# Query tiles 2 to 4 in float16 parts, late products ordered behind the feed-forward part's, and two unread products more

## The chip, the core and the metric

The kernel runs on one core of a Trainium2 chip. The core's engines have instruction queues of their own, each worked off in order: TensorE (PE in the profile; its weight loads are PEld), VectorE (DVE), ScalarE (ACT), GpSimd (POOL), and SyncE (SP), which issues the DMAs. They wait for one another by semaphores. The metric is the device time of one execution in microseconds; lower is better.

## The reference

Linear attention with softmax-like features, then a feed-forward layer over the attention's output.

```python
q, k, v: (8, 8, 576, 64)   omega: (128, 64)   w_in: (512, 2048)   w_out: (2048, 512)
def phi(x):                      # x scaled by 64 ** -0.25
    h = einsum('bhsd,md->bhsm', x, omega) - sum(x * x) / 2
    return exp(h - max(h, axis=-1)) / sqrt(128)
q_p, k_p = phi(q_s), phi(k_s)
kv  = einsum('bhsm,bhsd->bhmd', k_p, v);  z = sum(k_p, axis=2)
att = einsum('bhsm,bhmd->bhsd', q_p, kv) / (einsum('bhsm,bhm->bhs', q_p, z) + 1e-6)
x   = att as (4608, 512)
h   = x @ w_in
out = (h * tanh(softplus(h))) @ w_out
```

## The kernel before

The 4608 rows are 36 query tiles of 128 rows (`q_task`, tile t) and 18 feed-forward chunks of 256 rows (two tiles each). Per batch element b there are four tasks `k_task` (two heads each), whose result `kv` a query tile needs, and one `v_task` that finds the scale of v. Every tile or chunk goes through a list of steps, and a slot counter with numbers written by hand (`FIRST`, `GAP`, `pace`, the `yield` values) sets in which order the steps are written out. A scheduler then sets each engine's final order from that; a waiting instruction holds all behind it on its engine.

**Two kinds of product.** A product is done either in float32 or in float16 parts: the operand is rounded to float16, the rest is kept as a second float16 array, and three products (or two, for the features) add up. In parts, TensorE has more instructions, each much shorter; the splitting costs work on the other engines.

**A query tile** t below `QF` (5) runs in float32: the features `pq` (L333), a maximum `mxq` on VectorE, eight exponentials on ScalarE with the maximum as bias (L347), eight transposes `pt` on TensorE (L528), copies `qp` on ScalarE, the products `pn` with the float32 `kvf` (L539). From `QF` on it runs in parts: `sq` = the rounded q (ScalarE, L68) and its rest (GpSimd, L77), `pq` from these, `mxq` and the subtraction `eq` (L351) on VectorE, one exponential (L357), its two parts `qn` (ScalarE, VectorE), a transpose by DMA `qp<-qn` (L471), the products `pn` (L485) with `kv`. Either way follow the division into `x` on VectorE, its parts `xs`, and a transpose by DMA into `xT` of its chunk; for tiles 0 and 1 instead transposes `px` on TensorE (L563) into a float32 `xT`.

**A key task** gives `pk` (L333), `ek`, and then `pkv`: for b = 0 and 1 (`KF` = 2) in float32 (L403), later in parts with `vb` (L435), whose rest part is GpSimd's. `kv_parts` splits the `kvf` of b = 0 or 1 into `kv` for tiles in parts; with `QF` = 5 only b = 1 needs it.

**The scales.** `pow2` takes a maximum over all partitions with GpSimd's `partition_all_reduce` (L110): `allm_v` once for each b, `allm_w` once for each of the two weights. Between that operation and an ordinary one on GpSimd the program has an `ISA` instruction that changes GpSimd's library.

**The feed-forward part.** `ff_in` gives the products `ph` (L626) into two PSUM buffers, emptied by ScalarE; `ff_out` the products `po` (L669, L686). Chunk 0 is float32 (`wi0`, `wo0`); meanwhile ScalarE and VectorE unpack the weights (`w_task`: the Prelu of L178, the maxima `wmax`, the Abs of L192) and split them (`w_split`), which chunk 1 and later need. `mish` needs another function table on ScalarE than the exponentials and the rest; `mish0` does chunk 0's in one piece.

**Unread products.** `spin(n, left, right)` issues n products that nobody reads. `ps_a`, four PSUM buffers, holds `pq`, `pk`, `pt`, `pn`, `pkv` and `px` in turn.

Of the kernel before, what the change touches and what calls it, by code (L numbers as in the profile page):

```python
# [2 lines left out]

# [7 lines left out]
F32 = mybir.dt.float32  # L11
# [18 lines left out]
def tile_kernel(  # L30
# [129 lines left out]
    @contextmanager  # L160
    def behind(nth):
        with ExitStack() as st:
            for ins in anchors.get(nth, ()):
                st.enter_context(tc.issue_after(ins))
            yield

    def w_task(i, name):

        n = 0 if name == "wi" else 1
        raw = loaded.pop(f"w{n}_{i}", None) or fetch_w(n, i, w_dma)  # L170
        yield W_LOAD
        word = raw.bitcast(I32).rearrange("p (n two) -> p n two", two=2)
        low, high = word[:, :, 0], word[:, :, 1]
        dst = flat32(slots[w_at(n, i)])
        di = dst.bitcast(I32)
        with behind((AN, AO)[n][i]):
            m = high.bitcast(F32)
            act.activation(m, m, AF.Prelu, scale=2.0 ** -112, alpha=-(2.0 ** 32))  # L178
            dve.tensor_single_scalar(out=di, in_=low, scalar=29, op=ALU.logical_shift_right)
        yield W_GAP  # L180
        did("w", n, i)
        with behind((AN, AO)[n][i]):
            dve.scalar_tensor_tensor(
                out=di, in0=high, scalar=3, in1=di, op0=ALU.logical_shift_left, op1=ALU.bitwise_or
            )
            if n == 0:
                dve.tensor_reduce(
                    out=wmax[n][:, i:i + 1], in_=dst, axis=AX.X, op=ALU.max, apply_absolute_value=True
                )
            else:  # L190

                act.activation(m, dst, AF.Abs, accum_out=wmax[n][:, i:i + 1])  # L192
# [100 lines left out]
    unit = [0]  # L293

    loaded = {}
    anchors = {}
# [15 lines left out]
    def features(load, tiles, name, nth, whole):  # L312

        f = loaded.pop(name, None) or fetch(load, name)
        yield gap("load", name)
        if whole:

            terms = ((f, om_f[0:D]),)  # L320
        else:
            terms = yield from in_parts(f, name, nth)
        n = sum(len(g) for g in tiles)
        by_act = whole
        e = sb.tile([P, n, M], F32, tag="ae", name=f"e{name}", bufs=2)
        mx = sb.tile([P, n], F32, tag="mx", name=f"mx{name}")
        pps, lo = [], 0
        for g in tiles:
            pp = ps_a.tile([P, 4, M], F32, tag="a", name=f"p{name}_{lo}")
            for i, parts in enumerate(g):  # L330
                for rows, o in parts:
                    for j, (left, right) in enumerate(terms):
                        nc.tensor.matmul(  # L333
                            out=pp[rows, i, :], lhsT=left[:, o:o + rows.stop - rows.start],
                            rhs=right, start=j == 0, stop=j == len(terms) - 1,
                        )
# [25 lines left out]

    kvf = {}
# [18 lines left out]
    def k_task(nth, b, hp):  # L382
# [46 lines left out]
        rest(by("vlo", nth), v_lo, va, v_hi, s_v)  # L429
        yield gap("kv", f"k{b}_{hp}")  # L430
        pkv = ps_a.tile([P, 2, D1], F32, tag="a", name=f"pkv{b}_{hp}", padded_shape=[P, 2, 256])
        for j in range(2):
            mm = [(t, u, x, y) for x, y in ((1, 0), (0, 1), (0, 0)) for t, u in steps[j]]
            for i, (t, u, x, y) in enumerate(mm):
                nc.tensor.matmul(  # L435
                    out=pkv[:, j, :], lhsT=kp[:, x, t, :], rhs=vv[:, y, u, :],
                    start=i == 0, stop=i == len(mm) - 1,
                )
# [16 lines left out]
    def q_task(nth, t):  # L455
# [15 lines left out]
        nc.sync.dma_start_transpose(  # L471
            out=qp.rearrange("p a h s -> p (a h) s"), in_=qn.rearrange("p a h m -> p (a h m)")
        )
        yield 2
        x = sb.tile([P, H, D], F32, tag="x", name=f"x{t}", bufs=2)
        rd = sb.tile([P, H, 1], F32, tag="rd", name=f"rd{t}")
        pns = []
        for g in range(2):
            pn = ps_a.tile([P, 4, D1], F32, tag="a", name=f"pn{t}_{g}", padded_shape=[P, 4, P])
            for i in range(4):  # L480
                h = 4 * g + i
                for b, lo, hi in spans(t * P, P):
                    must(HP, "kv", b)
                    for n, (a, y) in enumerate(((1, 0), (0, 1), (0, 0))):
                        nc.tensor.matmul(  # L485
                            out=pn[lo:hi, i, :], lhsT=qp[:, a, h, lo:hi], rhs=kv[b][:, h, y, :],
                            start=n == 0, stop=n == 2,
                        )
            pns.append(pn)
# [31 lines left out]
    def q_first(nth, t, e, off):  # L521
# [11 lines left out]
        for g in range(2):  # L533
# [9 lines left out]
            dve.tensor_single_scalar(out=rd[:, hs], in_=pn[:, :, D:D1], scalar=EPS, op=ALU.add)  # L543
            dve.reciprocal(out=rd[:, hs], in_=rd[:, hs])
            if t * P < CH:
                xt = dve.tensor_tensor(
                    out=x[:, hs, :], in0=pn[:, :, 0:D], in1=rd[:, hs].broadcast_to([P, 4, D]),
                    op=ALU.mult,
                )
# [12 lines left out]
        for i in range(KT):  # L562
            nc.tensor.transpose(out=px[:, i, :], in_=x[:, 2 * i:2 * i + 2, :], identity=ident)  # L563
# [43 lines left out]
    def ff_in(c):  # L607
# [3 lines left out]
        for gr in range(FT // FG):  # L611
            gT[c, gr] = sb.tile([P, 2, FG, CH], F16, tag="g", name=f"g{c}_{gr}", bufs=GB)
            for q in range(FG // FQ):
# [4 lines left out]
                for j in range(0, FQ, 2):  # L618
                    ph = ps_h.tile([P, 2, CH], F32, tag="h", name=f"ph{c}_{gr}_{q}_{j}")
                    for i in range(2):  # L620
# [2 lines left out]
                        if c == 0:  # L623
                            mm = [(None, None, k) for k in range(KT)]
                        for n, (a, y, k) in enumerate(mm):
                            nc.tensor.matmul(  # L626
                                out=ph[:, i, :], lhsT=wi(a, k, f) if c else wi0(k, f),
                                rhs=xT[c][:, y, k, :] if c else xT0()[:, k, :],
                                start=n == 0, stop=n == len(mm) - 1,
                            )  # L630
# [48 lines left out]
    def ff_out0():  # L679

        po = [ps_o.tile([P, DM], F32, tag="o", name=f"po0_{i}") for i in range(CH // P)]
        for blk in reversed(range(NB)):
            for i in range(CH // P):
                for f in (2 * blk, 2 * blk + 1):
                    must(f // FG + 1, "g", 0, f % FG // FQ)
                    nc.tensor.matmul(  # L686
                        out=po[i], lhsT=g0(f // FG)[:, f % FG, i * P:(i + 1) * P], rhs=wo0(f),
                        start=blk == NB - 1 and f % 2 == 0, stop=blk == 0 and f % 2 == 1,
                    )
# [218 lines left out]
```

## Time and profile before

| | |
|---|---|
| three runs | 990.11, 991.0 and 972.43 us; median 990.11 us |
| profiled execution | 972.64 us, span 970.9 us, mean granted TensorE clock 0.987 |
| TensorE busy | 953.8 us, 98% of the span |
| ScalarE, VectorE, GpSimd busy | 642.4, 529.6, 218.0 us |
| the costliest groups on TensorE | `ph` in parts 379.9 us (3264 products), `po` in parts 373.1 us (1632) |

A row of a timeline has the start in us, the duration, the engine, the line, the operation, what it writes and reads, the shape, and the number of instructions merged; in square brackets the engine's idle time before it and what ended that. A row of a table by stretches has the stretch, its length, then the busy time of PE, PEld, DVE, ACT and POOL with the number of instructions in brackets, the granted TensorE clock (1.00 is full speed), the DMA share and GB/s. A row of waits has who waited, for whom, the sum in us, how often, and the longest. A float32 product counts twice on TensorE in the trace and once in the program's order.

### The profile page before, as it was taken

To read this page: it belongs to the slowest core of one execution; us is meant where nothing else is said; L and a number is where in the kernel's file an instruction comes from. 1 tells how busy PE (TensorE), PEld (TensorE's weight loads), DVE (VectorE), ACT (ScalarE), POOL (GpSimd) and SP (SyncE) were. 2 spreads that over 40 slices of the span, in tenths; PEclk is the share of its full clock that TensorE was granted. 3 is DMA by queue.
4 is the path that set the end of the run, shared out by engine and by line. 5 is a ranking of instruction groups with operands and counts; after the bars stand their busy time and mean duration, and the time that the engine had idled before them with its cause. 6 is when DMAs were issued, how large, how long until landed. Compare 5 with 4: busy or idle time off the path is not lost.

```text
span 970.9 us, 19229 instructions
## 1 busy us (share of the span) xinstructions
PE 953.8 (98%) x8184; PEld 684.0 (70%) x8184; DVE 529.6 (55%) x945; ACT 642.4 (66%) x838; POOL 218.0 (22%) x135
## 2 busy tenths in 40 slices
PE   8999998998999999999999999999999999999998
PEld 6788874775777777777777777777777777766663
DVE  5868676585656655655465665565546555211110
ACT  4659995797676867777667775877667766232230
POOL 0000051243222422322132323332223130000000
PEclk9979998999999999999999999999999999999999
DMA  9756323432441245322422253312530124200000
GB/s 289 263 204 209 108 73 67 101 80 63 98 107 37 83 93 111 63 67 73 112 57 59 63 119 73 89 37 68 90 89 24 45 55 88 44 23 11 12 12 32
DMA packets 122245, 82.21 MB, mean 85 GB/s; under 512 B 102832, under 2 KB 102960, under 8 KB 122160
## 3 DMA queue, kind: packets, MB, share of 16 engines
q1 hardware_dynamic: 122160, 80.99, 33.3%
q8 instruction: 64, 1.05, 0.4%
q14 instruction: 21, 0.17, 0.1%
HBM read 46.37 MB, written 9.44 MB: 57 GB/s over the span
## 4 chain that ended last, share of the span: by engine, by line
PE 75%; DVE 1%; issue 0%; POOL 0%; ACT 0%; ACTq 0%
PE po L669 34%; PE ph L626 32%; PE pk L333 3%; PE pq L333 2%; PE pn L485 2%; PE pkv L435 2%; POOL vb L77 0%; DVE g L79 0%; DVE eq L351 0%; DVE mxq L342 0%; ACT o L68 0%; DVE vb L70 0%; DVE kv L79 0%; DVE p_v L117 0%; DVE s_v L119 0%
## 5 line engine op out<-in xcount | busy, mean ns | idle before, releaser
L626 PE MATMUL ph<-xT,w 128*128 128x256 f16 (+1 forms) x3392 | 413.3, 278 | 0.7 <-ACT xT L68 0.7
L669 PE MATMUL po<-wo,g 128*128 128x512 f16 x1632 | 373.1, 379 | 0.0
L626 PEld LDWEIGHTS <-w 128*128 128x128 f16 x3264 | 318.4, 98 | 59.7 <-issue 0.8
L669 PEld LDWEIGHTS <-g 128*128 128x128 f16 x1632 | 155.7, 98 | 163.6
L645 ACT ACTIVATE h<-ph,us 128x512 f32<-128x512 f32 (+3 forms) x184 | 101.1, 574 | 199.3 <-PE ph L626 198.5
L79 DVE SCALAR_TENSOR_TENSOR g<-h,us,g 128x1024 f16<-128x1024 f32 (+3 forms) x92 | 112.5, 1238 | 118.1 <-ACT g L68 117.7
L77 POOL TENSOR_TENSOR sq<-fq,sq 64x1024 f16<-64x1024 f32 x31 | 71.6, 2309 | 178.6 <-issue 100.4
L77 POOL TENSOR_TENSOR sk<-fk,sk 64x1152 f16<-64x1152 f32 x24 | 59.2, 2468 | 116.2 <-DVE mxq L342 27.6
L68 ACT ACTIVATE g<-h,us 128x1024 f16<-128x1024 f32 (+3 forms) x92 | 82.4, 923 | 1.2
L77 POOL TENSOR_TENSOR xs<-x,xs 128x512 f16<-128x512 f32 x32 | 42.5, 1328 | 141.9 <-ACT h L645 47.1
L342 DVE TENSOR_REDUCE mxq<-pq 128x4 f32<-128x512 f32 x72 | 46.9, 684 | 49.4 <-PE pq L333 49.3
L645 ACT ACT_TABLE_LOAD x55 | 70.6, 1283 | 1.0
L357 ACT ACT_TABLE_LOAD x53 | 68.0, 1283 | 0.9
L342 DVE TENSOR_REDUCE mxk<-pk 128x4 f32<-128x512 f32 (+1 forms) x96 | 50.3, 550 | 33.4 <-PE pk L333 33.4
L77 DVE TENSOR_TENSOR qn<-eq,qn 128x1024 f16<-128x1024 f32 x31 | 39.9, 1286 | 50.4 <-ACT qn L68 50.4
L77 DVE TENSOR_TENSOR kp<-ek,kp 128x1152 f16<-128x1152 f32 x24 | 37.7, 1570 | 21.0 <-ACT kp L68 21.0
L77 POOL TENSOR_TENSOR vb<-vf,vb 128x640 f16<-128x640 f32 x24 | 39.8, 1661 | 30.5 <-DVE vb L70 18.4
L68 ACT ACTIVATE o<-po,us 128x512 f32<-128x512 f32 (+1 forms) x38 | 25.9, 682 | 30.9 <-PE po L669 30.8
L281 DVE TENSOR_REDUCE vmx<-vf 128x1 f32<-128x640 f32 x32 | 25.9, 816 | 35.5 <-DMA vf<-in_vL_dram 35.4
L351 DVE TENSOR_TENSOR eq<-pq,mxq 128x512 f32<-128x512 f32 x62 | 39.9, 681 | 0.0
L357 ACT ACTIVATE eq<-eq,lnt 128x1024 f32<-128x1024 f32 x31 | 35.6, 1149 | 6.2 <-DVE eq L351 5.9
L357 ACT ACTIVATE ek<-ek,lnt 128x1152 f32<-128x1152 f32 x24 | 30.1, 1256 | 12.3 <-DVE ek L351 12.1
(124 smaller groups left out, 920.5 us busy)
## 6 DMA issues: line engine op xcount, KB each, us to landing
vf<-in_vL_dram SPq DMA_DIRECT2D x32, 325.0 KB, 3.3
fk<-in_kT_dram SPq DMA_DIRECT2D x32, 288.0 KB, 3.6
fq<-in_qT_dram SPq DMA_DIRECT2D x36, 256.0 KB, 3.5
out_dram<-o SPq DMA_DIRECT2D x36, 256.0 KB, 2.3
raw<-in_w_out_dram SPq DMA_DIRECT2D x5, 1024.0 KB, 9.2
wo<-in_w_in_dram SPq DMA_DIRECT2D x4, 1024.0 KB, 13.2
raw<-in_w_in_dram SPq DMA_DIRECT2D x4, 1024.0 KB, 15.3
wo<-in_w_out_dram SPq DMA_DIRECT2D x3, 1024.0 KB, 7.0
```

The lines of the kernel that those rows point to most:

```text
L68: act.activation(out, in_, AF.Copy, scale=scale)
L77: eng.tensor_tensor(out=out, in0=in_, in1=hi, op=ALU.subtract)
L79: eng.scalar_tensor_tensor(out=out, in0=in_, scalar=scale, in1=hi, op0=ALU.mult, op1=ALU.subtract)
L281: dve.tensor_reduce(out=mx[:, hp:hp + 1], in_=vt[hp][:, :, 0:D], axis=AX.XY, op=ALU.max, apply_absolute_value=True,)
L333: nc.tensor.matmul(out=pp[rows, i, :], lhsT=left[:, o:o + rows.stop - rows.start], rhs=right, start=j == 0, stop=j == len(terms) - 1,)
L342: sub = dve.tensor_reduce(out=mx[:, lo:hi], in_=pp[:, :m, :], axis=AX.X, op=ALU.max, negate=by_act)
L351: sub = dve.tensor_tensor(out=e[:, lo:hi, :], in0=pp[:, :m, :], in1=mx[:, lo:hi].unsqueeze(2).broadcast_to([P, m, M]), op=ALU.subtract,)
L357: last = act.activation(e, e, AF.Exp, bias=lnt)
L435: nc.tensor.matmul(out=pkv[:, j, :], lhsT=kp[:, x, t, :], rhs=vv[:, y, u, :], start=i == 0, stop=i == len(mm) - 1,)
L626: nc.tensor.matmul(out=ph[:, i, :], lhsT=wi(a, k, f) if c else wi0(k, f), rhs=xT[c][:, y, k, :] if c else xT0()[:, k, :], start=n == 0, st ...
L645: act.activation(h[:, :, lo:hi], ph[:, :, lo:hi], AF.Mish, scale=us[:, 0:1])
L669: nc.tensor.matmul(out=po[i], lhsT=gT[c, gr][:, a, f % FG, i * P:(i + 1) * P], rhs=wo(y, f), start=f == 0 and (a, y) == parts[0], stop=f = ...
```

## The change

- `QF` goes from 5 to 2: tiles 2, 3 and 4 go the way in parts. With that `kv_parts` runs for b = 0 too.
- The products `pkv` in parts and `pn` in parts are traced in a block whose instructions are placed on TensorE behind the last `ph` or `po` written so far, and `pn` comes one slot later (`yield 3`).
- Two products `spin` of tile 0's `x` with `ident`, written behind tile 0's `px`.
- `anchors`, `behind`, `AN` and `AO` go; with `AN` and `AO` full of `None` they ordered nothing.

```diff
+    ff_mm = [None]
+    def behind_ff():
+        return tc.issue_after(ff_mm[0].ins) if ff_mm[0] is not None else ExitStack()
...
         pkv = ps_a.tile([P, 2, D1], F32, tag="a", name=f"pkv{b}_{hp}", padded_shape=[P, 2, 256])
-        for j in range(2):
+        with behind_ff():
+            for j in range(2):
...
-        yield 2
+        yield 3
         x = sb.tile([P, H, D], F32, tag="x", name=f"x{t}", bufs=2)
         rd = sb.tile([P, H, 1], F32, tag="rd", name=f"rd{t}")
         pns = []
-        for g in range(2):
+        with behind_ff():
+            for g in range(2):
...
         cast(act, xT0()[:, :, off:off + P], px)
+        if off == 0:
+            spin(2, ident, x[:, 0:4, :].rearrange("p h d -> p (h d)"))
         did("x", 0)
...
-                            nc.tensor.matmul(
+                            ff_mm[0] = nc.tensor.matmul(
                                 out=ph[:, i, :], lhsT=wi(a, k, f) if c else wi0(k, f),
...
-    KF, QF = 2, 5
+    KF, QF = 2, 2
```

What this does to the order shows best at three places; names carry the tile's number (`sq2` is tile 2, `pk1_0` is b = 1, task 0) and a counter.

The first place is where tile 2 meets the scale of w_in, on two engines. GpSimd, from the first scale of v on, before:

```order
L110 ISA allm_v0_166<-vam0_164 128x1
L110 ISA allm_w0_636<-am_w0_634 128x1
L110 ISA allm_v1_746<-vam1_744 128x1
L110 ISA allm_v2_1339<-vam2_1337 128x1
L110 ISA allm_w1_1102<-am_w1_1099 128x1
L77 ISA
L77 TENSOR_TENSOR sq5_1170<-fq5_1052,sq5_1170 64x1024
```

and now:

```order
L110 ISA allm_v0_166<-vam0_164 128x1
L77 ISA
L77 TENSOR_TENSOR sq2_532<-fq2_506,sq2_532 64x1024
L77 TENSOR_TENSOR sq3_534<-fq3_508,sq3_534 64x1024
L110 ISA
L110 ISA allm_w0_604<-am_w0_602 128x1
L110 ISA allm_v1_794<-vam1_792 128x1
L110 ISA allm_v2_1417<-vam2_1415 128x1
L77 ISA
L77 TENSOR_TENSOR sq4_1077<-fq4_999,sq4_1077 64x1024
L110 ISA
L110 ISA allm_w1_1120<-am_w1_1117 128x1
```

One change of the library (`L77 ISA`) became five up to `sq5` (a last `L77 ISA` follows the rows shown), and `sq4` and `allm_w1` now stand between two changes each.

VectorE at the same place, where the last piece of w_in is unpacked, before:

```order
L183 SCALAR_TENSOR_TENSOR w8_112<-raw7_155,w8_112 128x1024
L342 TENSOR_REDUCE mxq2_511<-pq2_4_517 128x4
L187 TENSOR_REDUCE wmax0_123<-w8_112 128x1
L342 TENSOR_REDUCE mxq3_523<-pq3_0_524 128x4
L203 TENSOR_REDUCE am_w0_634<-wmax0_123 128x1
```

and now:

```order
L180 SCALAR_TENSOR_TENSOR w8_112<-raw7_155,w8_112 128x1024
L79 SCALAR_TENSOR_TENSOR kv0_157<-kvf0_158,kvs0_495,kv0_157 128x8x64
L79 SCALAR_TENSOR_TENSOR kv0_157<-kvf0_158,kv0_157 128x8
L184 TENSOR_REDUCE wmax0_123<-w8_112 128x1
L338 TENSOR_REDUCE mxq2_539<-pq2_0_540 128x4
L200 TENSOR_REDUCE am_w0_602<-wmax0_123 128x1
```

The splitting of `kv0` (four rounds like the two rows shown, each with two roundings) stands between the pieces of w_in, and tile 2's first maximum came behind all of them.

The second place: TensorE, b = 1's key tasks, which in both programs come towards the end of chunk 0's `ph`, before:

```order
L333 MATMUL pk1_0_0_693<-om_f_97,fk1_0_666 128x128 x4
L333 MATMUL pk1_0_4_698<-om_f_97,fk1_0_666 64x128 x2
L333 MATMUL pk1_0_5_701<-om_f_97,fk1_0_666 128x128 x4
L626 MATMUL ph0_0_1_2_707<-xT0_307,w4_108 128x256 x8
L333 MATMUL pk1_1_0_756<-om_f_97,fk1_1_681 128x128 x4
L333 MATMUL pk1_1_4_761<-om_f_97,fk1_1_681 64x128 x2
L626 MATMUL ph0_1_0_0_773<-xT0_307,w5_109 128x256 x2
L333 MATMUL pk1_1_5_764<-om_f_97,fk1_1_681 128x128 x4
L626 MATMUL ph0_1_0_0_773<-xT0_307,w5_109 128x256 x6
L403 MATMUL pkv1_0_807<-vf1_0_656,ek1_0_691 128x65 x10
```

and now, right behind the `pn` of tiles 2 and 3:

```order
L329 MATMUL pk1_0_0_723<-om_f_97,fk1_0_640 128x128 x4
L329 MATMUL pk1_0_4_728<-om_f_97,fk1_0_640 64x128 x2
L329 MATMUL pk1_0_5_731<-om_f_97,fk1_0_640 128x128 x4
L329 MATMUL pk1_1_0_806<-om_f_97,fk1_1_655 128x128 x4
L329 MATMUL pk1_1_4_811<-om_f_97,fk1_1_655 64x128 x2
L329 MATMUL pk1_1_5_814<-om_f_97,fk1_1_655 128x128 x4
L398 MATMUL pkv1_0_857<-vf1_0_626,ek1_0_721 128x65 x10
```

The products of chunk 0 that stood between `pk1_0`, `pk1_1` and `pkv1_0` now come earlier, ahead of `pn`: 48 of its 64 `ph` stand ahead of `pk1_0`.

The third place: GpSimd again, where b = 2's fourth key task meets b = 3's scale, before:

```order
L77 TENSOR_TENSOR sq10_2383<-fq10_2261,sq10_2383 64x1024
L110 ISA
L110 ISA allm_v3_2744<-vam3_2742 128x1
L77 ISA
L77 TENSOR_TENSOR vb1_118<-vf2_3_1259,vb1_118 128x10x64
```

and now:

```order
L77 TENSOR_TENSOR sq10_2461<-fq10_2339,sq10_2461 64x1024
L77 TENSOR_TENSOR vb1_118<-vf2_3_1275,vb1_118 128x10x64
L110 ISA
L110 ISA allm_v3_2794<-vam3_2792 128x1
L77 ISA
L77 TENSOR_TENSOR sq11_2578<-fq11_2496,sq11_2578 64x1024
```

`vb1`, which `pkv2_3` reads, moved ahead of the two changes of the library.

More of the change, by code (lines that the diff above doesn't have):

```diff
@@ L1 @@
 import math
-from contextlib import ExitStack, contextmanager
+from contextlib import ExitStack
 import concourse.bass as bass
@@ L158, in fetch_w @@
         return raw
[L160 to L165, printed above, removed]
+    ff_mm = [None]
+    def behind_ff():
+        return tc.issue_after(ff_mm[0].ins) if ff_mm[0] is not None else ExitStack()
     def w_task(i, name):
@@ L175, in w_task @@
         di = dst.bitcast(I32)
[L176 to L179, printed above, removed]
+        m = high.bitcast(F32)
+        act.activation(m, m, AF.Prelu, scale=2.0 ** -112, alpha=-(2.0 ** 32))
+        dve.tensor_single_scalar(out=di, in_=low, scalar=29, op=ALU.logical_shift_right)
         yield W_GAP
         did("w", n, i)
-        with behind((AN, AO)[n][i]):
-            dve.scalar_tensor_tensor(
-                out=di, in0=high, scalar=3, in1=di, op0=ALU.logical_shift_left, op1=ALU.bitwise_or
-            )
[L186 to L192, printed above, removed]
+        dve.scalar_tensor_tensor(
+            out=di, in0=high, scalar=3, in1=di, op0=ALU.logical_shift_left, op1=ALU.bitwise_or
+        )
+        if n == 0:
+            dve.tensor_reduce(
+                out=wmax[n][:, i:i + 1], in_=dst, axis=AX.X, op=ALU.max, apply_absolute_value=True
+            )
+        else:
+            act.activation(m, dst, AF.Abs, accum_out=wmax[n][:, i:i + 1])
     def w_at(n, i):
@@ L295, in tile_kernel @@
     loaded = {}
-    anchors = {}
     def fetch(load, name, tag="af", bufs=2):
@@ L341, in features @@
             m = hi - lo
-            sub = dve.tensor_reduce(
+            dve.tensor_reduce(
                 out=mx[:, lo:hi], in_=pp[:, :m, :], axis=AX.X, op=ALU.max, negate=by_act
@@ L346, in features @@
                 for i in range(m):
-                    last = act.activation(
+                    act.activation(
                         e[:, lo + i, :], pp[:, i, :], AF.Exp, bias=mx[:, lo + i:lo + i + 1]
@@ L350, in features @@
             else:
-                sub = dve.tensor_tensor(
+                dve.tensor_tensor(
                     out=e[:, lo:hi, :], in0=pp[:, :m, :],
@@ L356, in features @@
         if not by_act:
-            last = act.activation(e, e, AF.Exp, bias=lnt)
+            act.activation(e, e, AF.Exp, bias=lnt)
         elif nth < 6:
             spin(2, ident, e[:, 0:2, :].rearrange("p n m -> p (n m)"))
-        anchors[nth] = (last.ins, sub.ins)
         return e
@@ L431, in k_task @@
         pkv = ps_a.tile([P, 2, D1], F32, tag="a", name=f"pkv{b}_{hp}", padded_shape=[P, 2, 256])
-        for j in range(2):
[L433 to L438, printed above, removed]
+        with behind_ff():
+            for j in range(2):
+                mm = [(t, u, x, y) for x, y in ((1, 0), (0, 1), (0, 0)) for t, u in steps[j]]
+                for i, (t, u, x, y) in enumerate(mm):
+                    nc.tensor.matmul(
+                        out=pkv[:, j, :], lhsT=kp[:, x, t, :], rhs=vv[:, y, u, :],
+                        start=i == 0, stop=i == len(mm) - 1,
+                    )
         did("u", nu)
@@ L477, in q_task @@
         pns = []
-        for g in range(2):
[L479 to L489, printed above, removed]
+        with behind_ff():
+            for g in range(2):
+                pn = ps_a.tile([P, 4, D1], F32, tag="a", name=f"pn{t}_{g}", padded_shape=[P, 4, P])
+                for i in range(4):
+                    h = 4 * g + i
+                    for b, lo, hi in spans(t * P, P):
+                        must(HP, "kv", b)
+                        for n, (a, y) in enumerate(((1, 0), (0, 1), (0, 0))):
+                            nc.tensor.matmul(
+                                out=pn[lo:hi, i, :], lhsT=qp[:, a, h, lo:hi], rhs=kv[b][:, h, y, :],
+                                start=n == 0, stop=n == 2,
+                            )
+                pns.append(pn)
         yield 1
@@ L500, in q_task @@
             dve.reciprocal(out=rd[:, hs], in_=rd[:, hs])
-            xt = dve.tensor_tensor(
+            dve.tensor_tensor(
                 out=x[:, hs, :], in0=pn[:, :, 0:D], in1=rd[:, hs].broadcast_to([P, 4, D]),
@@ L504, in q_task @@
             )
-        anchors[30 + t] = (xt.ins,)
         yield from x_parts(nth, t, x)
@@ L545, in q_first @@
             if t * P < CH:
-                xt = dve.tensor_tensor(
+                dve.tensor_tensor(
                     out=x[:, hs, :], in0=pn[:, :, 0:D], in1=rd[:, hs].broadcast_to([P, 4, D]),
@@ L551, in q_first @@
             for b, lo, hi in spans(t * P, P):
-                xt = dve.scalar_tensor_tensor(
+                dve.scalar_tensor_tensor(
                     out=x[lo:hi, hs, :], in0=pn[lo:hi, :, 0:D], scalar=vstate[b][2][lo:hi],
@@ L555, in q_first @@
                 )
-        anchors[30 + t] = (xt.ins,)
         if t * P >= CH:
@@ L668, in ff_out @@
                     for a, y in parts:
-                        nc.tensor.matmul(
+                        ff_mm[0] = nc.tensor.matmul(
                             out=po[i], lhsT=gT[c, gr][:, a, f % FG, i * P:(i + 1) * P],
@@ L685, in ff_out0 @@
                     must(f // FG + 1, "g", 0, f % FG // FQ)
-                    nc.tensor.matmul(
+                    ff_mm[0] = nc.tensor.matmul(
                         out=po[i], lhsT=g0(f // FG)[:, f % FG, i * P:(i + 1) * P], rhs=wo0(f),
@@ L711, in tile_kernel @@
     W_LOAD, W_GAP, PRIO = 1, 1, 400
-    AN = (None,) * 8
-    AO = (None,) * 8
     W_LO = ('dddddddd', 'dddddddd')
```

1 line of the change is left out of this document (removed).

## The prediction

> **What bounds the kernel now.** I read the engines' shares first, then TensorE's waits, then the granted clock by stretches, then the timelines of GpSimd and TensorE where a wait stands. The shares and the waits from 60 us on:
>
> ```profile
> PE 953.8 (98%) x8184; PEld 684.0 (70%) x8184; DVE 529.6 (55%) x945; ACT 642.4 (66%) x838; POOL 218.0 (22%) x135
> PE pkv L435 <- POOL vb L77: 4.4, 1, 4.4
> PE pn L485 <- DMA qp<-qn: 3.4, 1, 3.4
> ```
>
> TensorE never stops but for two waits, so the end is its work, these waits, and what a low clock adds. The stretches with a low clock and those ahead of them, and ScalarE's share of one stage:
>
> ```profile
> 42.03:45.44 3.41, 2.16 (x18) 1.71 (x17) 3.19 (x11) 2.05 (x3) 0.00 (x0) 1.00 0.21 76
> 45.44:59.10 13.66, 12.97 (x46) 10.95 (x46) 13.07 (x21) 1.74 (x5) 0.35 (x1) 0.50 0.48 151
> 147.87:151.28 3.41, 1.06 (x3) 0.19 (x1) 3.33 (x4) 1.46 (x2) 0.00 (x0) 1.00 0.70 131
> 154.69:158.10 3.41, 3.41 (x12) 1.86 (x10) 3.33 (x7) 2.51 (x3) 1.34 (x1) 0.50 0.00 0
> 229.79:233.20 3.41, 1.57 (x12) 0.77 (x11) 3.01 (x6) 3.39 (x6) 0.00 (x0) 1.00 0.00 0
> 233.20:236.61 3.41, 0.84 (x26) 0.84 (x26) 0.00 (x0) 2.01 (x2) 2.20 (x2) 1.00 0.00 0
> 60.28:108.57 48.29, 48.24 (x309) 41.63 (x307) 35.95 (x67) 43.66 (x94) 0.35 (x1) 1.00 0.58 190
> ```
>
> The clock goes in steps of 3.41 us. It fell to half behind steps in which TensorE was busy for 0.84, 1.06 and (transposes among it) 2.16 us, and held behind one with 1.57. From 45.44 to 59.10 it ran at half, about 6.8 us lost. And from 60.28 to 108.57 ScalarE is busy for 43.66 of 48.29 us: the second engine there is close behind the first.
>
> **Part 1: TensorE's work.** The rows of a product of each kind, in chunk 0's stage and behind it:
>
> ```profile
> 29.20 3.83 PE L333 MATMUL pq<-om_f,fq 64*128 64x128 f32 x32
> 37.47 1.08 PE L528 MATMUL pt<-ident,eq 128*128 128x128 f32 x8
> 45.26 0.53 PE L563 MATMUL px<-ident,x 128*128 128x128 f32 x2 [1.02 <-DVE x L546]
> 47.62 7.19 PE L333 MATMUL pq<-om_f,fq 64*128 64x128 f32 x32
> 64.67 3.68 PE L539 MATMUL pn<-kvf,qp 128*128 128x65 f32 x32
> 72.66 2.61 PE L333 MATMUL pk<-om_f,fk 64*128 64x128 f32 x20
> 105.43 2.34 PE L403 MATMUL pkv<-vf,ek 128*128 128x65 f32 x20
> 115.12 2.05 PE L333 MATMUL pq<-om_f,fq 64*128 64x128 f32 x16
> 124.13 1.88 PE L686 MATMUL po<-wo,g 128*128 128x512 f32 x4
> 126.06 1.15 PE L539 MATMUL pn<-kvf,qp 128*64 128x65 f32 x32
> 169.62 0.91 PE L485 MATMUL pn<-kv,qp 128*128 128x65 f16 x24
> 172.16 1.06 PE L333 MATMUL pq<-om,sq 128*128 128x128 f16 x16
> 173.05 2.78 PE L626 MATMUL ph<-xT,w 128*128 128x256 f16 x24
> ```
>
> Removed for tiles 2 to 4, at full clock: 3.83 + 2.05 for `pq`, 3 x 1.08 for `pt`, 3.68 + 1.15 for `pn`, 13.95 us. Added: 3 x 1.06, 2 x 0.91, and tile 4's 48 half-height products at 0.91 / 24 each, 1.8: 6.8 us. Net -7.1 us. The two `spin` add about 1.1 us (four passes over 256 columns each, against 128 in `pq`'s row) in and around the wait of 1.02 at 45.26. If TensorE alone set the pace, -7.1 and, with the clock kept at 45 us, another -6.8 would be the gain.
>
> **Part 2: the other engines up to 108 us.** That gain is not let through. Tile 2's first maximum now stands behind all of w_in's unpacking and `kv0`'s splitting on VectorE; the pieces:
>
> ```profile
> 50.84 0.68 DVE L179 TENSOR_SCALAR w<-raw 128x1024 int32<-128x1024 int32 x1
> 52.04 1.21 DVE L183 SCALAR_TENSOR_TENSOR w<-raw,w 128x1024 int32<-128x1024 int32 x1
> 53.78 1.21 DVE L187 TENSOR_REDUCE wmax<-w 128x1 f32<-128x1024 f32 x1
> 120.25 0.48 DVE L72 TENSOR_SCALAR kv<-kvf,kvs 128x512 f16<-128x512 f32 x1
> 120.77 0.75 DVE L79 SCALAR_TENSOR_TENSOR kv<-kvf,kvs,kv 128x512 f16<-128x512 f32 x1
> 60.28 0.60 ACT L68 ACTIVATE g<-ph 128x512 f32<-128x512 f32 x1 [6.91 <-PE ph L626]
> 113.62 1.28 ACT L178 ACT_TABLE_LOAD   x1
> ```
>
> From 44.5 us (tile 1's `x`) there are four rounds of `kv0` (about 1.3 each), three pieces (3.0 each with their maximum) and one maximum more, with a step about 0.07 shorter than a duration: 14.6 us, to 59.1; then `mxq` and `eq`, to 61.7. ScalarE can start on tile 2 there, 1.5 us later than its row at 60.28. From there to the last copy of chunk 0 it loses, by the steps of its timeline, 12 short exponentials (0.25 each), four `qp`, one Prelu and two copies, 7 us, and gains two long exponentials and two `qn` (about 1 each), two table loads (1.28) and half of `mish0` (1.9), 8.5 us. Without any idle time it would end at 61.7 + 43.7 + 1.5, 107; before, 108.57. Its waits are added: a piece of w_out now stands on SP behind tile 2's transpose, another behind tile 4's load that waits for `pk1_2`; I put 2.5 us on both. So chunk 0 ends at about 109.5, and chunk 1's first `ph`, which waits for an earlier copy, starts at 107.7 as before (107.61). TensorE's gain becomes idle time between 68 and 98 us: `ph0_1_0_2` waits for a copy that stands behind five splittings, `pn` of tile 3 for its transpose (2.65 and 3.2 us by the same list), and `pk1_0`, `pk1_1`, `pkv1_0` have no `ph` between them.
>
> **Part 3: GpSimd's library.** What one change costs:
>
> ```profile
> 111.67 0.35 POOL L110 PARTITION_ALL_REDUCE allm_v<-vam  x1 [34.81 <-DVE vam L288]
> 121.96 0.35 POOL L110 PARTITION_ALL_REDUCE allm_w<-am_w  x1 [9.93 <-DVE am_w L206]
> 129.16 2.13 POOL L77 TENSOR_TENSOR sq<-fq,sq 64x1024 f16<-64x1024 f32 x1 [6.86 <-issue]
> 226.95 0.38 POOL L110 PARTITION_ALL_REDUCE allm_v<-vam  x1 [6.74 <-ACT g L68]
> 234.33 1.39 POOL L77 TENSOR_TENSOR vb<-vf,vb 128x640 f16<-128x640 f32 x1 [7.00 <-issue]
> qp<-qn SPq DMA_TRANSPOSE x31, 4.3
> ```
>
> Each change is 6.7 to 7.0 us. The first of the new ones is over long before `sq2`; the second ends at about 59.7, as the last maximum does. The other three stand in a row from 112.0: 6.86 and 2.13 (`sq4`, 121.0), 6.74 and 0.35 (`allm_w1`, 128.1 for 121.96 before), 6.86 and 2.13: `sq5` at 137.1. TensorE comes to `pq5` at 107.7 plus `pkv` 2.3, 163 `ph` at 2.62 / 24, seven `po` at 0.94, and `pq4` 0.9: 135.3, and waits 1.8. Behind `pq5` follow 0.5, 1.8, 2.6 and eleven `po`, 10.3: 153.2. Tile 5's `qn` and its transpose, behind tile 4's on SP, land at about 154.9 (4.3 from issue), a wait of 1.7 for the 3.4 of before. With 0.8, 0.9 and fourteen `po` chunk 2 starts at 169.8, and with `pn6` and `pq7`, still to come, at 171.4 in before's count: 173.05 there. Term: **-1.7**. The Trainium skill ("GPSIMD Engine Reference", 2.1 Instruction dispatch) puts the first call behind a library load at about 6 us; by that the row of three changes ends 2.6 us earlier, `pq5` waits no longer, and the sum is about 2 us lower. The rows are longer than that figure in this trace.
>
> **Part 4: the wait at 231 us.** `pkv2_3` waits for `vb`, which stood behind two changes (226.95 and 234.33 above); it now stands ahead of them.
>
> ```profile
> 235.77 0.96 PE L435 MATMUL pkv<-vb,kp 128*128 128x65 f16 x25 [4.41 <-POOL vb L77]
> 236.57 4.45 PE L626 MATMUL ph<-xT,w 128*128 128x256 f16 x24
> 256.07 1.23 SPq L515 DMA_TRANSPOSE xT<-xs  x1
> 279.62 2.78 PE L626 MATMUL ph<-xT,w 128*128 128x256 f16 x24
> ```
>
> The wait goes, 4.4, and with it the 1.7 that the half clock added to the next 24 `ph` (4.45 for 2.78). Next late is `sq11`, behind the changes, at about 240; its `pq` stands some 20 us of TensorE work further on. Term: **-6.1**. Behind that TensorE is busy throughout and its list differs only in `pn`, one `po` later (2.6 us). Tile 9's `xT` is issued at 256.07 and chunk 4 starts at 279.62: 20 us of cover, so nothing. Without that cover each chunk would wait up to 2.6.
>
> **Part 5: the clock in the new gaps.** With 2.16 us busy and `spin` filling the gap, I expect full clock at 45 us. But between 75.2 and 86.5 us TensorE has by the list 0.75 us of `pn` and 3.5 us of `pk`, products of 64 rows, and a step of `pq` of that kind at full occupation (47.62, 7.19) did not bring the clock back. So it falls at about 80. If `pkv1_0` and what follows bring it back after 6 us (as behind the wait at 149, where it was back at 158.10), the list ends 2.4 us later; if it stays at half until `ph` comes in a row, near 107, `pk1_2` takes 4.7 for 2.5 and `pkv1_1` about 4 for 2.2, ScalarE waits for both, and it is 9.5 us later, which part 3's row passes on. A gain has no ground. The nearest row is that of 154.69:158.10, so nearer the low end: **+4**.
>
> **Sum.** The profiled execution took 972.6 (span 970.9 and 1.7 around it): 972.6 - 1.7 - 6.1 + 4 = 968.8, said as **969**. It is near the lowest of the three runs shown (972.43); the median, 990.11, lies 1.8% above it.
>
> **Rivals.** *The clock holds.* No loss in part 5: 964.8. Against it stand the steps with 0.84 and 1.06. The Trainium skill ("TensorE: Matmul & The Clock Gate", Why this matters for your kernels) asks for no idle gap above about 3 us between bursts; by that gaps of 2.65 and 3.2 hardly touch the clock and this rival holds. The trace does not agree: the clock fell at 45.44 with no gap above the 1.02 us of the row at 45.26. *TensorE's saving is let through*: ScalarE and GpSimd keep up, and the wait at 149 with its half clock (3.4 and 3.4) goes too: 972.6 - 7.1 - 6.8 - 6.8 - 6.1 = 945.8; for it speaks that ScalarE idles 4.6 us in that stage, against it the order of its queue. *Slower: the clock stays at half from 80 to 107*: 972.6 - 1.7 - 6.1 + 9.5 = 974.3; it decides from 7.8 us of loss on. *The unread products don't hold the clock*: then `ph0_0_1_0` and the copies behind it come 4 us later and all behind them, 973.
>
> **Chances.** Forecast 0.40, clock holds 0.20, saving let through 0.13, half clock to 107 0.20, unread products of no use 0.07. The range leaves out most of the third, so it starts at 954; its upper end is not set by these cases but by the runs shown, which spread over 18.6 us for one kernel: 969 + 18.6, 988. A measurement of this kernel can tell about 2% from no change: faster by more (below 953) 0.15, within 0.79, slower 0.06.
>
> **What would show it.** Half clock gone at 45 to 59; TensorE idle between 68 and 98 with the clock at half from about 80; the first `ph` of chunk 1 at 107 to 112; five library gaps of about 6.8 on GpSimd before `sq5`; `pq5` at about 137; no wait on `vb`. Wrong it would be if chunk 1 starts before 104, or if a chunk waits for `xT`.

## The result

The changed kernel takes 983.7 to 985.7 us, the kernel before 972.4 beside it on the same chip: ratio **1.0125, 95% interval 1.0096 to 1.0154**. Both kernels also have executions some 18 us longer at a lower granted clock; the comparisons here leave them out, and the profiled executions of f32_no_spin and tile4_vector are of that kind, so only their ratios are used. The time lies in the forecast's range, but the sign is the other one: 0.4% faster was forecast, and 1.25% slower came.

The changed kernel's shares, from its page, and its TensorE waits:

```profile
PE 954.3 (97%) x8196; PEld 683.6 (70%) x8196; DVE 529.9 (54%) x969; ACT 646.5 (66%) x821; POOL 225.9 (23%) x138
...
PE ph L623 <- ACT g L68: 6.3, 1, 6.3
PE pq L329 <- POOL sq L77: 4.5, 4, 1.7
PE pn L482 <- DMA qp<-qn: 6.7, 3, 3.5
```

The wait for `vb` is gone, as forecast. But TensorE is busy for 954.3 us, 0.5 more than before, though about 7 us of products net were taken out: what was saved in products went into a slower clock. The stretches of the changed kernel, in the order of the prediction's table:

```profile
45.44:59.10 13.66, 10.97 (x72) 9.28 (x73) 13.66 (x18) 5.40 (x7) 5.43 (x2) 1.00 0.52 157
60.28:108.57 48.29, 39.62 (x208) 34.21 (x207) 39.86 (x75) 37.28 (x66) 0.73 (x2) 0.70 0.62 176
86.40:106.88 20.48, 20.25 (x89) 18.15 (x88) 15.01 (x26) 15.37 (x42) 0.00 (x0) 0.50 0.50 134
168.32:171.74 3.42, 3.42 (x37) 3.14 (x35) 2.44 (x8) 1.71 (x2) 0.00 (x0) 0.56 0.00 0
188.80:192.22 3.42, 3.42 (x27) 2.77 (x26) 3.06 (x7) 2.70 (x3) 1.44 (x1) 0.56 0.02 5
```

The half clock at 45 to 59 us is gone (1.00). From 60 to 108 us, where the clock was 1.00, it is 0.70, and from 86.4 to 106.9 it is 0.50 although TensorE is busy for 20.25 of 20.48 us there. ScalarE is busy for 15.37 of that stretch: it no longer holds the stage. TensorE does, at half speed. Cut where the clock changes, the stage is:

```profile
72.34:79.17 6.83, 4.96 (x32) 4.15 (x33) 6.56 (x8) 5.95 (x8) 0.00 (x0) 0.50 0.99 267
82.58:85.99 3.41, 2.38 (x34) 2.00 (x31) 2.97 (x8) 3.39 (x4) 0.00 (x0) 1.00 0.75 293
85.99:109.88 23.89, 23.66 (x98) 21.02 (x98) 15.42 (x27) 18.42 (x47) 0.00 (x0) 0.50 0.49 131
```

The clock fell twice: at 72.3, in the wait of 6.30 us for `g`, and was back after two steps; and at 86.0, and then stayed at half for seven. TensorE's timeline there, with the waits in square brackets:

```profile
74.21 1.22 PE L623 MATMUL ph<-xT,w 128*128 128x256 f32 x2 [6.30 <-ACT g L68]
...
82.22 0.92 PE L482 MATMUL pn<-kv,qp 128*128 128x65 f16 x24 [1.12 <-DMA qp<-qn]
...
91.89 4.53 PE L398 MATMUL pkv<-vf,ek 128*128 128x65 f32 x20
96.35 4.69 PE L329 MATMUL pk<-om_f,fk 64*128 64x128 f32 x20
100.97 2.07 PE L623 MATMUL ph<-xT,w 128*128 128x256 f32 x4
102.84 4.37 PE L398 MATMUL pkv<-vf,ek 128*128 128x65 f32 x20
107.00 4.23 PE L623 MATMUL ph<-xT,w 128*128 128x256 f32 x12
...
119.43 0.82 PE L623 MATMUL ph<-xT,w 128*128 128x256 f16 x6
```

The key tasks' `pk` and `pkv` take 4.4 to 4.7 us where the prediction's rows show 2.61 and 2.34. Only behind the twelve rows of `ph` (six products) that start at 107 is the clock back, at 109.9. Chunk 1's first `ph` starts at 119.43, before at 107.61: **+11.8 us**, and the span grew by 11.0 in all. From there to chunk 2's first `ph` it is 63.7 us (65.4 before), and from that to the end of the span 798.8 (797.9 before).

### The profile page after: what moved, and what is told of

The parts are those of the page before. It is cut to its first block, busy times and chain, and to the rows that moved or that the text cites. A ratio compares the mean times of both kernels' runs of the same rounds, so it can differ in the third digit from the quotient of the medians.

```text
span 981.9 us, 19284 instructions
## 1 busy us (share of the span) xinstructions
PE 954.3 (97%) x8196; PEld 683.6 (70%) x8196; DVE 529.9 (54%) x969; ACT 646.5 (66%) x821; POOL 225.9 (23%) x138
## 4 chain that ended last, share of the span: by engine, by line
PE 70%; ACT 1%; DVE 0%; issue 0%; ACTq 0%
PE po L666 32%; PE ph L623 30%; PE pk L329 2%; PE pq L329 2%; PE pkv L431 2%; PE pn L482 2%; DVE g L79 0%; ACT L642 0%; ACT g L68 0%; ACT eq L353 0%; ACT qn L68 0%; ACT h L642 0%; ACT o L68 0%; DVE x L498 0%; DVE rd L497 0%
## 5 line engine op out<-in xcount | busy, mean ns | idle before, releaser
L79 DVE SCALAR_TENSOR_TENSOR g<-h,us,g 128x1024 f16<-128x1024 f32 (+3 forms) x92 | 101.2, 1111 | 122.0 <-ACT g L68 122.0
L77 POOL TENSOR_TENSOR sq<-fq,sq 64x1024 f16<-64x1024 f32 x34 | 79.2, 2331 | 201.8 <-issue 93.4
L77 POOL TENSOR_TENSOR xs<-x,xs 128x512 f16<-128x512 f32 x32 | 40.2, 1255 | 195.1 <-issue 140.0
L77 POOL TENSOR_TENSOR sk<-fk,sk 64x1152 f16<-64x1152 f32 x24 | 60.2, 2510 | 78.0 <-ACT sk L68 28.7
L77 DVE TENSOR_TENSOR qn<-eq,qn 128x1024 f16<-128x1024 f32 x34 | 43.3, 1273 | 55.4 <-ACT qn L68 55.4
L77 DVE TENSOR_TENSOR kp<-ek,kp 128x1152 f16<-128x1152 f32 x24 | 37.4, 1557 | 30.7 <-ACT kp L68 30.7
L353 ACT ACTIVATE eq<-eq,lnt 128x1024 f32<-128x1024 f32 x34 | 39.0, 1148 | 13.3 <-DVE eq L347 12.9
L77 POOL TENSOR_TENSOR vb<-vf,vb 128x640 f16<-128x640 f32 x24 | 39.6, 1655 | 21.8 <-DVE vb L70 14.5
L347 DVE TENSOR_TENSOR eq<-pq,mxq 128x512 f32<-128x512 f32 x68 | 43.6, 681 | 0.0
L329 PE MATMUL pq<-om,sq 128*128 128x128 f16 x544 | 37.8, 225 | 4.5 <-POOL sq L77 4.5
```

The costliest lines, as they stand in the source:

```text
L77: eng.tensor_tensor(out=out, in0=in_, in1=hi, op=ALU.subtract)
L79: eng.scalar_tensor_tensor(out=out, in0=in_, scalar=scale, in1=hi, op0=ALU.mult, op1=ALU.subtract)
L329: nc.tensor.matmul(out=pp[rows, i, :], lhsT=left[:, o:o + rows.stop - rows.start], rhs=right, start=j == 0, stop=j == len(terms) - 1,)
L347: dve.tensor_tensor(out=e[:, lo:hi, :], in0=pp[:, :m, :], in1=mx[:, lo:hi].unsqueeze(2).broadcast_to([P, m, M]), op=ALU.subtract,)
```

## Experiments

Three theories for the 11 to 12 us (the expectations call b = 1 "sequence 1"). **Theory 1, the clock**: the float16 tiles empty TensorE at 68 to 86 us, the clock falls, and the sparse products of b = 1's key tasks, now without `ph` between them, don't bring it back. **Theory 2**: GpSimd's added library changes. **Theory 3**: the order behind the feed-forward products and the later `pn`. Ratios are to the kernel before; runs sent together share its executions.

**1. f32_tiles: tiles 2 to 4 in float32 again, the rest of the change kept.**

```diff
-    KF, QF = 2, 2
+    KF, QF = 2, 5
```

> Tiles 2 to 4 stay in float32 as before; the order behind the feed-forward products, the later pn and the two unread products stay. Theory 1 (clock: the loss is the half clock in the key stage of sequence 1, which the float16 tiles opened by emptying TensorE there): no half clock between 60 and 108 us, chunk 1's first ph at 101 to 108, time 1 to 8 us under the kernel before (ratio 0.992 to 0.999). Theory 2 (GpSimd's library changes for sq2 to sq4): the same, since those are gone too. Theory 3 (the order: products held behind the feed-forward part's): the loss stays, ratio 1.008 to 1.015.

Ratio 0.992 (0.9894 to 0.9946); chunk 1's first `ph` at 104.72, and its stretch, by the same columns:

```profile
86.30:108.00 21.70, 21.70 (x152) 19.01 (x150) 14.35 (x26) 18.03 (x39) 0.00 (x0) 1.00 0.51 161
```

Full clock in that stretch, no loss: theory 3 falls, and the loss comes with the float16 tiles. It doesn't tell theory 1 from theory 2.

**2. hold_k1 and hold_pn3_k1: unread products to hold the clock.** In both, the key tasks of b = 1 get two each; in the second four more, float16 products of a constant tile `idle`, go behind tile 3's `pn`.

```diff
-        elif nth < 6:
+        elif nth < 12:
             spin(2, ident, e[:, 0:2, :].rearrange("p n m -> p (n m)"))
...
+        if t == 3:
+            with tc.issue_after(mm.ins):
+                spin(4, idle[:, 0:P], idle)
```

> The changed kernel with two more unread products (1.1 us at full clock) behind each of the four key tasks of sequence 1, as the tasks of sequence 0 have them. Theory 1 (clock): they bring the clock back at 89 to 93 us in place of 108, chunk 1's first ph moves from 119.4 to 111 to 114, time 5 to 9 us under the changed kernel, ratio to the kernel before 1.003 to 1.007. If two are too few: half clock as before, chunk 1 at 120 to 121, ratio 1.012 to 1.015. Theory 2 (library changes) and theory 3 (order): clock back, but chunk 1 earlier by less than 3 us and ratio 1.010 to 1.015.

> As hold_k1, and four unread float16 products of 512 columns (1.6 us at full clock) right behind tile 3's pn, ahead of pk1_0, where the clock fell. Theory 1: the clock does not fall at 86 at all, chunk 1's first ph at 109 to 112, time 7 to 11 us under the changed kernel, ratio 1.001 to 1.005. Theories 2 and 3: ratio 1.010 to 1.015.

Ratios 1.0148 (1.0128 to 1.0168) and 1.014 (1.012 to 1.0159). The first is the case "two are too few"; for the second my number was wrong (the four took 1.02 us, not the 1.6 I had put). The stretches, first of hold_k1, then of hold_pn3_k1:

```profile
86.40:113.71 27.31, 27.04 (x103) 22.68 (x102) 16.37 (x27) 18.66 (x46) 0.00 (x0) 0.51 0.48 119
```

```profile
84.64:88.05 3.41, 3.00 (x26) 2.47 (x24) 3.29 (x9) 3.40 (x7) 0.00 (x0) 1.00 0.58 139
88.05:91.47 3.42, 3.42 (x12) 2.27 (x13) 3.19 (x6) 3.23 (x10) 0.00 (x0) 0.50 0.76 163
```

In hold_pn3_k1 the step ahead of the fall holds almost nothing but `pk`: TensorE was busy for 3.00 of 3.41 us, and the clock fell, where 1.57 us of other products held it in the prediction's table. Busy time alone doesn't decide. In hold_k1 two unread products per task did not bring the clock back either. Neither run kept it, so neither tests theory 1.

**3. lo_on_vector: GpSimd does no `sq2` to `sq4`.**

```diff
-        rest(by("lo", nth), ks[D:P], f, ks[0:D])
+        rest(dve if nth < 13 else by("lo", nth), ks[D:P], f, ks[0:D])
```

> The changed kernel with the lower parts of sq2 to sq4 on VectorE, so that GpSimd changes its library once less at each of the first two and once less at sq4. Theory 2 (library): the waits of pq2 to pq4 for sq (4.5 us together) go, sq5 comes some 13 us earlier, chunk 2 starts 3 to 8 us earlier, ratio 1.004 to 1.009. Theory 1 (clock): half clock between 86 and 108 stays, chunk 1's first ph stays within 2 us of 119.4, and the gain is what sq5 alone gives, 0 to 3 us: ratio 1.009 to 1.013. Theory 3: 1.010 to 1.015.

Ratio 1.0107 (1.0082 to 1.0131): as theory 1 said, not theory 2. The library changes for `sq2` to `sq4` are gone, the half clock stays and chunk 1's first `ph` is at 120.99. The roundings went to VectorE, so the run doesn't test the library changes alone: the wait of 6.30 us for `g` is gone, and those for the transposes grew from 6.7 to 16.4. Its waits:

```profile
PE pn L482 <- DMA qp<-qn: 16.4, 5, 6.6
PE pq L329 <- POOL sq L77: 2.7, 1, 2.7
```

**4. hold_f16: dense unread products that wait for nothing**, eight behind tile 3's `pn`, four each behind `pk1_0` and `pk1_1`.

```diff
+        if nth in (8, 9):
+            with tc.issue_after(mm.ins):
+                spin(4, idle[:, 0:P], idle)
...
+        if t == 3:
+            with tc.issue_after(mm.ins):
+                spin(8, idle[:, 0:P], idle)
```

> The changed kernel with unread float16 products of 512 columns behind tile 3's pn (eight, 1.7 us) and behind pk1_0 and pk1_1 (four each, 0.9 us): dense products that need nothing and so fill the gaps at 82 to 87 us. Theory 1 (clock): the clock stays full from 83 us on, the stage loses 10.7 us of half clock and pays about 2 us of added work, chunk 1's first ph at 109 to 113 (119.4 in the changed kernel), ratio to the kernel before 1.001 to 1.007. If another engine holds chunk 0 (ScalarE's queue): full clock, but TensorE idles in its place, chunk 1 at 116 to 120, ratio 1.010 to 1.015. If sparse products of key tasks let the clock fall even so: half clock as before, chunk 1 at 120 to 122, ratio 1.013 to 1.017.

Ratio 1.0041 (1.0001 to 1.008): two thirds of the loss are gone though 4 us of TensorE work were added. Its stretch and timeline:

```profile
86.30:108.00 21.70, 21.33 (x166) 17.04 (x167) 19.13 (x36) 21.04 (x48) 0.00 (x0) 1.00 0.65 192
```

```profile
78.95 1.22 PE L629 MATMUL ph<-xT,w 128*128 128x256 f32 x2 [6.30 <-ACT g L68]
...
87.43 1.89 PE L93 MATMUL spin<-idle 128*128 128x512 f16 x8
89.25 2.61 PE L329 MATMUL pk<-om_f,fk 64*128 64x128 f32 x20
91.79 1.04 PE L93 MATMUL spin<-idle 128*128 128x512 f16 x4
...
115.13 2.78 PE L629 MATMUL ph<-xT,w 128*128 128x256 f16 x24
```

This profiled execution starts the stage 4.7 us late (78.95 for 74.21; half clock at 18 to 28 us in its key tasks of b = 0), so I read the distance: from that `ph` to chunk 1's first it takes 36.2 us, in the changed kernel 45.2. The clock is worth 9.0 us, net of the added products. ScalarE is now nearly as full there as TensorE (21.04 and 21.33 of 21.70). The expectation's 109 to 113 us is met with the 4.7 taken off: 110.4. All library changes and the order are still in this run, so theories 2 and 3 don't explain its gain. Theory 1 is shown.

**5. What the change's other parts do**, on f32_tiles: without the order behind the feed-forward products; with `pn` at two steps again; without the two unread products. And no_spin, the changed kernel without these two.

```diff
-        return tc.issue_after(ff_mm[0].ins) if ff_mm[0] is not None else ExitStack()
+        return ExitStack()
...
-        yield 3
+        yield 2
...
-        if off == 0:
-            spin(2, ident, x[:, 0:4, :].rearrange("p h d -> p (h d)"))
```

> As f32_tiles, without the order behind the feed-forward products (pkv and pn may go ahead again); pn one step later and the two unread products stay. If that order took away the wait of 4.4 us for vb at 231 us with its half clock (6.1 us in all): the wait is back, ratio 0.996 to 1.000. If the order does nothing there and the earlier start alone moved vb ahead of the library change: no wait, ratio 0.990 to 0.995.

> As f32_tiles, with pn two steps behind its transpose again, not three. If the later pn is what moved vb ahead of the library change: the wait of 4.4 us for vb at 231 us is back, with 1.7 us of half clock, ratio 0.996 to 1.001. If it is another part: no wait for vb, ratio 0.990 to 0.995.

> As f32_tiles, without the two unread products between the x tiles. If they gave the full clock at 45 to 59 us: half clock from 45.4 to 59 as in the kernel before, chunk 1's first ph at 106.5 to 108.5 (104.7 in f32_tiles), ratio to the kernel before 0.994 to 0.998. If the gain of f32_tiles is the order's alone: chunk 1 at 104 to 106 and ratio 0.990 to 0.994.

> The changed kernel without the two unread products between the x tiles. Half clock from 45.4 to 59 us as in the kernel before. If ScalarE's and VectorE's queues hold chunk 0 (part 2 of the prediction): chunk 1's first ph stays within 2 us of 119.4, ratio 1.010 to 1.015. If TensorE's work is on the path there: chunk 1's first ph at 123 to 126, ratio 1.016 to 1.021.

f32_no_behind: 0.9906 (0.9872 to 0.9941), no wait for `vb`: the order is worth nothing that can be measured. f32_pn_step2: 0.9969 (0.9943 to 0.9995), and its wait is back, with a longer `ph` behind it:

```profile
236.13 1.54 PE L431 MATMUL pkv<-vb,kp 128*128 128x65 f16 x25 [5.52 <-POOL vb L77]
237.47 3.64 PE L623 MATMUL ph<-xT,w 128*128 128x256 f16 x24
```

So with float32 tiles it is the later `pn` that takes this wait away. f32_no_spin: 0.9936 (0.9912 to 0.996), at the border of its two expectations, which the interval doesn't tell apart, and not apart from f32_tiles. no_spin: 1.0141 (1.0102 to 1.0179), chunk 1's first `ph` at 120.78, but against the expectation the clock is full at 45 to 59 us:

```profile
45.44:59.10 13.66, 10.71 (x72) 9.00 (x72) 13.66 (x19) 5.33 (x7) 5.43 (x2) 1.00 0.50 148
```

In f32_tiles, which has both unread products, the same stretch ran at 0.75. In the changed kernel they weren't needed. Dense `ph` stand there now in place of tile 2's 64-row `pq`; that this is why was not tried by itself.

**6. f16_old_order: the kernel before with the float16 tiles and nothing else.**

```diff
-    KF, QF = 2, 5
+    KF, QF = 2, 2
```

> The kernel before with tiles 2 to 4 in float16 parts and nothing else of the change: pn two steps behind its transpose, no order behind the feed-forward products, no unread products between the x tiles. If the loss is the float16 tiles' alone and the rest of the change gains what it gained in f32_tiles (8 us): ratio 1.016 to 1.024. If the later pn or the order emptied TensorE in the key stage: full clock there, ratio 0.990 to 1.005.

Ratio 1.0123 (1.0081 to 1.0165), so the sum I expected was wrong: the parts don't add up. The loss is there in full without the order and the later `pn`, with half clock from 84.4 to 104.8 us; and there is no wait for `vb` either, which f32_pn_step2 has. The float16 tiles take that wait away by themselves, so beside them the later `pn` has nothing to give.

**7. f16_tile4 and tile4_vector: only tile 4 in float16 parts** (`QF` = 4), in the second with `sq4`'s rest on VectorE.

```diff
-    KF, QF = 2, 2
+    KF, QF = 2, 4
...
-        rest(by("lo", nth), ks[D:P], f, ks[0:D])
+        rest(dve if nth < 13 else by("lo", nth), ks[D:P], f, ks[0:D])
```

> The changed kernel with tiles 2 and 3 in float32 as before and tile 4 alone in float16 parts. Theory 1 (the loss comes from tiles 2 and 3, whose float16 parts empty TensorE at 68 to 86 us): full clock from 60 to 108, chunk 1's first ph at 104 to 108, ratio 0.988 to 0.998. If tile 4's part (three library changes in a row ahead of sq5, a late transpose) has a loss of its own: chunk 1 at 104 to 108 but chunk 2's first ph more than 66 us behind it, ratio 0.998 to 1.006.

> As f16_tile4 (tiles 2 and 3 in float32, tile 4 in float16 parts), with sq4's lower part on VectorE, so that GpSimd changes its library once, not three times, between allm_v1 and sq5. Theory 2, here for chunk 1's stage alone: pq5's wait for sq5 (3.8 us, and some 1.5 us of half clock behind it) goes, ratio to the kernel before 0.988 to 0.993, a version faster than both. If tile 5's transpose takes the wait's place: ratio 0.993 to 0.998.

Ratios 0.9956 (0.9926 to 0.9986) and 0.9958 (0.9938 to 0.9979). In f16_tile4 chunk 1's first `ph` is at 104.56 and chunk 2's 63.9 us later: tiles 2 and 3 made the loss, and tile 4's stage has none of its own. The clock is not quite full ahead of it, against the expectation: 0.90 from 86.40 to 103.46, one step at half around a wait of 1.31 us for `g`. TensorE still waits 3.8 us for `sq5`:

```profile
136.52 1.73 PE L329 MATMUL pq<-om,sq 128*128 128x128 f16 x16 [3.81 <-POOL sq L77]
```

Taking two library changes away from in front of `sq5` gained nothing that can be measured beside f16_tile4. The ratio is that of the second case of the expectation, in which tile 5's transpose takes the wait's place; that it does is not shown. All six versions with tiles 2 and 3 in float32 (f32_no_behind, f32_tiles, f32_no_spin, f16_tile4, tile4_vector, f32_pn_step2) beat both kernels, with ratios from 0.9906 to 0.9969.

## Why the prediction was wrong

The forecast was 968.8 and the profiled execution 983.7, 14.9 more. By stages: chunk 1 starts at 119.4 where the sum had 111.7 (107.7 and +4), 7.7; from there to chunk 2 63.7 us where the steps had 62.1, 1.6; from chunk 2 to the span's end 798.8 where they had 793.3 (970.9 - 1.7 - 6.1, less 169.8), 5.5. That makes 14.8; the rest is rounding.

- **Part 5, the step that failed.** That the clock falls in the gaps was right; that `pkv1_0` and what follows bring it back after 6 us was wrong. It stayed at half for 23.9 us, from 86.0 to 109.9. So the term was mis-sized: +4 taken, 11.7 came (119.4 - 107.7), of which hold_f16 shows 9.0 to be the clock; the other 2.7 are not taken apart. The fault was the choice of the nearest row. 154.69:158.10, where the clock came back after one full step, was full of `po` with 512 columns, as the timeline of the kernel before shows; `pk` and `pkv` have 64 rows or 65 columns:

```profile
155.28 5.06 PE L686 MATMUL po<-wo,g 128*128 128x512 f32 x8
```

The row for these stood in the same table, 45.44:59.10 with 12.97 of 13.66 busy at half clock: 7.19 us of `pq` with 64 rows (47.62) did not bring the clock back, the `ph` behind them did, by 59.10:

```profile
54.75 5.43 PE L626 MATMUL ph<-xT,w 128*128 128x256 f32 x14
```

The text used this row for the fall but not for the return. By that row the "slower" rival, not the forecast, was the likeliest. That rival is what happened, and even its price, +9.5, was low.
- **Part 1** was right in its products but for tile 4's 48 half-height ones, which took 0.96 us where 1.8 was put, and the clock held at 45 us, but not by the two unread products (no_spin). "That gain is not let through" was right.

```profile
151.22 0.96 PE L482 MATMUL pn<-kv,qp 128*64 128x65 f16 x48
```

- **Part 2** was right in direction and short by some 3.5 us: VectorE's list put tile 2's first maximum at 59.1, and it came at 62.59; ScalarE began tile 2's exponential at 65.41 for 61.7. The copy of `g` stands behind eight pieces of that queue, whence 6.30 us of wait where 2.65 was forecast:

```profile
65.41 1.15 ACT L353 ACTIVATE eq<-eq,lnt 128x1024 f32<-128x1024 f32 x1 [3.77 <-DVE eq L347]
...
73.59 0.57 ACT L68 ACTIVATE g<-ph 128x512 f32<-128x512 f32 x1
```

The 3.5 us come from two roundings of `kv0` on VectorE. They took 2.61 and 2.11 us while GpSimd worked on `sq2` and `sq3`; their like took 0.75 and 0.19 some ten us later, about what the list had for them:

```profile
47.92 5.43 POOL L77 TENSOR_TENSOR sq<-fq,sq 64x1024 f16<-64x1024 f32 x2 [26.30 <-ACT sq L68]
48.76 2.61 DVE L79 SCALAR_TENSOR_TENSOR kv<-kvf,kvs,kv 128x512 f16<-128x512 f32 x1
51.30 2.11 DVE L79 SCALAR_TENSOR_TENSOR kv<-kvf,kv 128x8 f16<-128x8 f32 x1
60.72 0.75 DVE L79 SCALAR_TENSOR_TENSOR kv<-kvf,kvs,kv 128x512 f16<-128x512 f32 x1
61.38 0.19 DVE L79 SCALAR_TENSOR_TENSOR kv<-kvf,kv 128x8 f16<-128x8 f32 x1
```

In lo_on_vector, where GpSimd does nothing there, all four rounds take 0.75 and 0.19; in f16_old_order, no_spin and hold_f16, where it does, one round takes 2.60 and 2.11 again.

- **Part 3** was near up to `pq5` (30.3 us behind chunk 1's start, 29.4 in the working), and wrong behind it: tile 5's `pn`, held by its transpose, came 48.4 us behind chunk 1's start where the working had 47.2, and TensorE was there at 44.9 for 45.5.

```profile
140.37 0.38 POOL L110 PARTITION_ALL_REDUCE allm_w<-am_w  x1 [6.10 <-issue]
147.50 5.20 POOL L77 TENSOR_TENSOR sq<-fq,sq 64x1024 f16<-64x1024 f32 x2 [6.75 <-DVE g L79]
149.68 1.07 PE L329 MATMUL pq<-om,sq 128*128 128x128 f16 x16 [0.98 <-POOL sq L77]
```

```profile
167.85 1.49 PE L482 MATMUL pn<-kv,qp 128*128 128x65 f16 x24 [3.50 <-DMA qp<-qn]
...
187.17 0.92 PE L482 MATMUL pn<-kv,qp 128*128 128x65 f16 x24 [2.11 <-DMA qp<-qn]
```

The wait of 1.7 became 3.50 with a step of half clock behind it (0.56 at 168.32), and tile 6's, which I hadn't priced, 2.11 with another (0.56 at 188.80). With a wait of 1.46 for tile 11's `x` at 294 us, the second makes up most of the 5.5 behind chunk 2. This part rests on the trace alone; it wasn't tried. The Trainium skill ("GPSIMD Engine Reference", 2.1 Instruction dispatch) has about 6 us for a first call behind a library load; the rows here show 6.1 to 6.75.
- **Part 4** came as forecast: no wait at 231 us. Which part of the change did it was left open there; the runs say that either the float16 tiles or the later `pn` is enough.
- **The clock rule**, which the prediction weighed for the gaps alone. The Trainium skill ("TensorE: Matmul & The Clock Gate", What's actually happening) has full clock after one busy window of about 3.4 us. By that the half clock of 86.0 would have ended one step later, at 89.4, and chunk 1 would have started near 109 (an estimate: the 20.5 us that were left to 109.9 would have taken half as long), below the 111.7 of the sum. The trace does not agree: from 86.40 to 106.88, six steps in a row filled with `pk`, `pkv` and four rows of `ph` (two products; 20.25 of 20.48 us busy), it stayed at 0.50.

## What to carry over

Before taking products off TensorE, look at what stands next to the sparse ones (few rows, few columns): dense products between them carry the clock, and moving those away can cost more than the products saved. Price half clock by the row with the same kind of product, for the fall and for the return. Ask of a list of one engine's pieces what a second engine does beside them: two short roundings became 3.8 us longer here. When a change bundles several parts, measure them apart: here the small ones alone gave 0.8%, with the large one 1.25% was lost.

## What was not expected of the hardware

The same mix of sparse products can keep a full clock and yet not bring back a lost one. In the key tasks of b = 0, two steps full of `pk`, `pkv` and a few unread products ran at full clock in the changed kernel, and at half in hold_f16's profiled execution; first the changed kernel, then hold_f16:

```profile
21.55:24.96 3.41, 3.41 (x27) 2.82 (x26) 2.99 (x9) 3.23 (x10) 0.07 (x1) 1.00 1.05 386
24.96:28.38 3.42, 3.42 (x32) 3.22 (x29) 3.42 (x5) 2.81 (x9) 0.00 (x0) 1.00 1.05 387
```

```profile
21.55:24.96 3.41, 3.41 (x17) 3.19 (x16) 2.75 (x7) 2.25 (x6) 0.00 (x0) 0.50 1.05 388
24.96:28.38 3.42, 3.42 (x13) 2.59 (x12) 0.00 (x0) 0.37 (x2) 0.00 (x0) 0.52 1.05 386
```

TensorE is busy throughout in both; at half clock it gets through about half as many products per step (17 and 13 for 27 and 32). That fits a count of work done rather than of busy time, with a mix that lies above the count at full clock and below it at half; this reading was not tested by itself. Nor is it settled how much dense work brings the clock back: in f16_old_order it was back at 104.8, behind a step of four rows of `ph` and then `pkv`, where the changed kernel's step of `pk` and the same four did not do it.
